# A fused attention and gated-MLP kernel: new instruction orders, and a first x load cut into single blocks on one queue

## The chip, the cores and the metric

One core of a Trainium2 chip runs the whole kernel in one launch. The metric is device time in microseconds (us), the median of several runs; a profile of one more execution goes with it. TensorE multiplies matrices, VectorE and ScalarE move results out of PSUM and do the elementwise work, GpSimd builds masks and copies some weights, SyncE issues most DMAs. Each engine runs its own list of instructions in order; semaphores tie the lists together.

## The reference, cut to what matters

x has 2048 tokens of 448 numbers (bf16). Four layers follow each other: attention (layer 0), gated MLP (1), attention (2), gated MLP (3), with the same weights for the two of a kind.

```
x = x + A(layernorm(x))     # q, k, v = x @ wqkv, 16 heads of 28;
                            # each token sees 8 keys: itself and those 2, 4, ... 14 tokens before
                            # softmax over the 8, times v, then @ wo
x = x + B(layernorm(x))     # ((x @ w_gate) * (x @ w_up)) @ w_down, 1792 wide, no activation
x = x + A(layernorm(x))
x = x + B(layernorm(x))
```

## The kernel before, in words

**Tiling.** Tokens stand in 16 blocks of 128; x stays in SBUF in x_sb, even tokens in blocks 0 to 7, odd tokens in 8 to 15, so that a dilation of 2 becomes a plain window of 8. A layer is cut into chunks of 256 or 512 tokens. SEQ interleaves the chunks of the four layers, since a chunk of the next layer can start as soon as its blocks of x are done.

**LayerNorm** (`ln_chunk`): for each block, statistics on VectorE (L580, L582), Ln and Exp on ScalarE for rstd (L583, L585), scaling on VectorE into xn_sb (L601), then a transpose. For layer 0 the transpose is done by TensorE (L611 for the first two blocks, L615) and copied out of PSUM by ScalarE or VectorE (L622, L625). For layers 1 to 3 it is a DMA transpose issued from the sync queue (L604), into xnTa for attention and xnTb for the MLP.

**Attention.** `qk_chunk`: Q and K for a chunk in four units, copied to qk (L710). `v_group`: V for pairs of query blocks of 120 tokens (L775 to L802); the last four heads of V go by DRAM (vt) and come back by a DMA transpose (L730). `attn_front`, for a group of two query blocks: masked Q (L821), an S burst of 64 small matmuls (L833), two exps on ScalarE (L842), two minima with the mask on VectorE (L849). `attn_back`: an AV burst of 64 small matmuls (L867), copies, a shuffle of the sums (L892), Ln and Exp for their reciprocal (L893, L894) and the product into oT (L905). `y_blocks`: the output projection of two blocks (Y), added to x by L922.

**MLP** (`b_chunk`): 14 gate/up units of a chunk. Each is seven steps of two matmuls on xnTb and WGU; ScalarE copies gate to g_sb (L958), VectorE multiplies with up into hT (L961). Then w_down for two blocks (on WD and hT), added to x by L922. The last two blocks of the last layer have matmuls of the full height (L973), block 14 whole, block 15 in two halves of 224 columns, added by L977 and stored.

**Steps and bursts.** Most matmuls use 64 rows, so two run at once: a step. A product of this kind has a first and a second half, in which the two row halves of the array change roles. Line L348 issues such a step. While a burst runs, steps of one other product can be issued in strips of 32 columns (L351) between its small matmuls.

**What sets the order.** The functions only declare operations, numbered as declared. ORDER (L101) gives for each engine the numbers in the order in which they are issued; `46` is one operation, `a+b/h` or `a*3/h` are strips of a set between the matmuls of burst h. BANKS gives the PSUM banks of each product. Both were written by a planner outside of the kernel, with an assumed duration for each operation. `schedule` lays the operations out by these lists, `emit` puts in a wait wherever an operation needs another engine's result or a bank that is still in use. The sync queue's DMAs stand in such a list too, so a DMA that waits holds those behind it.

**The first loads** (`load_x` and `plain_dma`, L440 to L467): x blocks 0 and 1 in one load, 2 and 3 in one, then 4 to 7, 8 to 11, 12 to 15; the Q and K columns of wqkv in four loads to a staging area (stg 0 to 3), the V columns in two (wv), the last V heads in two small ones (stv). Eight copies (L519) bring the staged weights into WQK, spaced by 32. Loads stg 0 and stg 2 are issued by ScalarE, all others by SyncE in the order x 0-1, x 2-3, x 4-7, wv, wv, stg 3, stg 1, x 8-11, x 12-15. Warm-up matmuls (L511) on zeros keep TensorE busy until the first transposes.

```
def load_x(q, lo=0, hi=4):
    two, b0 = q // 2, 4 * (q % 2)
    plain_dma("sp", x_sb[:, 4 * q + lo:4 * q + hi, :], x_par[two][:, b0 + lo:b0 + hi, :], ...)
```

Of the kernel before, what the change touches and what calls it, by code (L numbers as in the profile page):

```python
# [8 lines left out]
D = 448  # L9
# [84 lines left out]
def grp_nc(g):  # L94
# [21 lines left out]
    ),  # L116
    "act": (
# [12 lines left out]
    ),  # L130
    "dve": (
# [18 lines left out]
    ),  # L150
    "pool": (
        "23 27 34 38 39 20 28 17 19 18 43 22 21 67 68 63 24 64 25 35 26 36 31 29 30 71 73 77 75 74 32 33 40 41 42 37"
    ),
# [223 lines left out]
def build(nc, A_x, A_wqkv, A_wo, B_w_gate, B_w_up, B_w_down, out):  # L377
# [68 lines left out]
    def load_x(q, lo=0, hi=4):  # L446
        two, b0 = q // 2, 4 * (q % 2)
        plain_dma("sp", x_sb[:, 4 * q + lo:4 * q + hi, :], x_par[two][:, b0 + lo:b0 + hi, :], [("x", -1, B) for B in range(4 * q + lo, 4 * q + hi)],
                  f"d_x{q}" + "h" * (lo > 0), prio=XP_[q + (q > 0 or lo > 0)])

# [653 lines left out]
```

## Time and profile before

| | us |
|---|---|
| median of 3 runs | 390.66 (390.62 to 390.84) |
| profiled execution | 391.03 |
| its span, first to last instruction | 389.3 |
| TensorE busy in it | 379.0 |
| VectorE busy | 290.3 |
| ScalarE busy | 203.2 |
| GpSimd busy | 9.7 |

The profiled execution has 1.7 us around its span. PE is TensorE, PEld its weight loads, DVE VectorE, ACT ScalarE, POOL GpSimd, SPq the sync queue. A line of a timeline has the start, the length (of several merged instructions where a count stands behind it), engine, line, operation, what it writes and reads, and in square brackets how long the engine had stood idle before and what ended that. A matmul's busy time holds the way through the array, so two rows' lengths overlap; where a step's cost is wanted, starts are compared with starts. A wait for several things is put down to the one that came last by the profile.

### The profile page before, as it was taken

The page shows a single profiled execution, that of the slowest core. Times are in us where ns is not written, and L with a number is a line of the kernel's source. Part 1 is how long each engine was busy: PE and PEld are TensorE (multiplying, and loading weights), DVE is VectorE, ACT ScalarE, POOL GpSimd, SP SyncE. Part 2 cuts the span into 40 slices and gives each one's busy share as a digit, 9 for nine tenths or more (in the row PEclk, how much of TensorE's full clock was granted, in tenths as well). Part 3 has the DMA queues.
Part 4 walks back from the last instruction along what each step waited for, and adds up shares of the span by engine and source line. Part 5 has one row for each costly group of instructions (what it writes and reads, how often), then busy time and mean ns, then how long its engine had stood idle before and what let it go on. Part 6 is the DMA issues. An engine that isn't in the chain of part 4 may idle for free.

```text
span 389.3 us, 14648 instructions
## 1 busy us (share of the span) xinstructions
PE 379.0 (97%) x6508; PEld 212.8 (55%) x6508; DVE 290.3 (75%) x640; ACT 203.2 (52%) x388; POOL 9.7 (2%) x40
## 2 busy tenths in 40 slices
PE   7999989989999999999999999999999999999997
PEld 2644567534555554545666577645555445544774
DVE  6988879978988897677766798466997777457333
ACT  4978875574655643445344555437764723243320
POOL 4220000000000000000000000000000000000000
DMA  8756151500632113042012303430116003203012
GB/s 274 170 146 179 28 150 49 101 12 2 96 30 44 27 25 60 16 57 49 2 22 42 67 2 62 70 52 14 24 29 88 17 2 49 50 2 96 3 37 71
DMA packets 54866, 22.52 MB, mean 58 GB/s; under 512 B 44996, under 2 KB 54804, under 8 KB 54804
## 3 DMA queue, kind: packets, MB, share of 16 engines
q1 hardware_dynamic: 54372, 21.08, 26.6%
q8 instruction: 51, 0.84, 0.9%
q10 hardware_dynamic: 432, 0.52, 0.4%
q14 instruction: 11, 0.09, 0.1%
HBM read 8.54 MB, written 2.71 MB: 29 GB/s over the span
## 4 chain that ended last, share of the span: by engine, by line
PE 90%; DMA 3%; DVE 3%; ACT 2%; issue 1%; SPq 0%
PE ps L348 82%; PE ps L351 3%; PE ps L833 2%; PE ps L867 2%; ACT E_sb L842 2%; PE ps L973 1%; DMA x_sb<-in_A_x_dram 1%; DMA xnTb<-xn_sb 1%; DMA xnTa<-xn_sb 1%; DVE xn_sb L601 1%; DVE st L580 1%; DVE E_sb L849 0%; PE ps L615 0%; ACT g_sb L958 0%; ACT v_sb L802 0%
## 5 line engine op out<-in xcount | busy, mean ns | idle before, releaser
L348 PE MATMUL ps<-xnTb,WGU 64*128 64x512 bf16 (+1 forms) x1944 | 177.7, 333 | 2.6 <-DMA xnTb<-xn_sb 1.3
L348 PEld LDWEIGHTS ps<-xnTb,WGU 64*128 64x128 bf16 x1944 | 94.9, 94 | 76.0 <-DMA xnTb<-xn_sb 1.6
L958 ACT ACTIVATE g_sb<-ps 128x512 bf16<-128x512 f32 (+1 forms) x140 | 69.6, 509 | 102.4 <-PE ps L348 87.7
L961 DVE TENSOR_TENSOR hT<-g_sb,ps 128x512 bf16<-128x512 bf16 (+1 forms) x140 | 77.9, 574 | 48.0 <-ACT g_sb L958 44.2
L348 PE MATMUL ps<-WD,hT 64*128 64x448 bf16 x766 | 79.0, 350 | 0.5 <-issue 0.3
L348 PEld LDWEIGHTS ps<-WD,hT 64*128 64x128 bf16 x766 | 36.1, 94 | 32.8 <-issue 1.3
L348 PE MATMUL ps<-xnTa,WQK 64*128 64x512 bf16 (+1 forms) x488 | 52.5, 352 | 0.5 <-ACT E_sb L842 0.2
L842 ACT ACTIVATE E_sb<-ps,shift_sb 128x1024 bf16<-128x1024 f32 (+1 forms) x36 | 37.2, 1068 | 19.7 <-PE ps L833 19.4
L922 DVE TENSOR_TENSOR x_sb<-x_sb,ps 128x448 bf16<-128x448 bf16 x62 | 36.8, 614 | 11.8 <-PE ps L348 11.7
L580 DVE BATCH_NORM_STATS2 st<-x_sb 128x6 f32<-128x448 bf16 x64 | 38.4, 615 | 2.9 <-DMA x_sb<-in_A_x_dram 2.5
L601 DVE TENSOR_SCALAR xn_sb<-x_sb,mv,rstd 128x512 bf16<-128x512 bf16 (+1 forms) x64 | 35.4, 571 | 4.4 <-ACT rstd L585 4.0
L348 PEld LDWEIGHTS ps<-xnTa,WQK 64*128 64x128 bf16 x488 | 22.8, 94 | 20.5 <-PE ps L348 1.8
L348 PE MATMUL ps<-wo_g,oT 64*128 64x448 bf16 x256 | 29.2, 349 | 0.1
L849 DVE TENSOR_TENSOR E_sb<-E_sb,MK 128x1024 bf16<-128x1024 bf16 (+1 forms) x36 | 23.3, 659 | 5.4 <-ACT E_sb L842 5.2
L710 ACT ACTIVATE qk<-ps 128x1024 bf16<-128x1024 f32 (+1 forms) x25 | 22.4, 920 | 8.6 <-PE ps L348 8.3
L905 DVE TENSOR_TENSOR oT<-O_sb,R_sb 128x480 bf16<-128x480 f32 (+3 forms) x36 | 21.8, 623 | 4.0 <-ACT R_sb L894 3.8
L893 ACT ACTIVATE R_sb<-R_sb 128x480 f32<-128x480 f32 (+1 forms) x34 | 20.1, 600 | 8.5 <-DVE R_sb L892 8.5
L892 DVE STREAM_SHUFFLE R_sb<-O_sb 128x480 f32<-128x480 f32 (+1 forms) x34 | 23.3, 694 | 0.1
L348 PE MATMUL ps<-WV,xnTa 64*128 64x336 bf16 (+3 forms) x244 | 22.5, 304 | 0.1
L878 ACT ACTIVATE O_sb<-ps 128x512 f32<-128x512 f32 (+2 forms) x22 | 11.9, 562 | 17.3 <-PE ps L867 17.2
L894 ACT ACTIVATE R_sb<-R_sb 128x480 f32<-128x480 f32 (+1 forms) x34 | 20.2, 602 | 0.6
L348 PEld LDWEIGHTS ps<-wo_g,oT 64*128 64x128 bf16 x256 | 12.4, 94 | 11.8 <-PE ps L348 0.5
(64 smaller groups left out, 228.2 us busy)
## 6 DMA issues: line engine op xcount, KB each, us to landing
out_dram<-x_sb SPq DMA_DIRECT2D x15, 112.0 KB, 1.8
x_sb<-in_A_x_dram SPq DMA_DIRECT2D x3, 448.0 KB, 6.3
WGU<-in_B_w_gate_dram SPq DMA_DIRECT2D x4, 224.0 KB, 3.6
WGU<-in_B_w_up_dram SPq DMA_DIRECT2D x4, 224.0 KB, 3.7
WD<-in_B_w_down_dram SPq DMA_DIRECT2D x2, 448.0 KB, 4.1
WGU<-in_B_w_gate_dram SPq DMA_DIRECT2D x2, 336.0 KB, 5.1
WGU<-in_B_w_up_dram SPq DMA_DIRECT2D x2, 336.0 KB, 5.1
WD<-in_B_w_down_dram SPq DMA_DIRECT2D x2, 336.0 KB, 3.8
```

The costliest lines, as they stand in the source:

```text
L348: return lambda E: E.matmul(out(), lhs(), rhs(), start=start, stop=stop)
L580: sc.add("dve", one(lambda E, B=B: E.bn_stats(st6[:, B, :], x_sb[:, B, :]), ("bn", li, B)), 525.0, deps=[("x", li - 1, B)] + ([("xn", li - ...
L601: sc.add("dve", one(lambda E, B=B, dst=dst, src=src: E.tensor_scalar(dst, src, mv[:, B, 0:1], rstd[:, B:B + 1], ALU.subtract, ALU.mult), ( ...
L710: return E.activation(dst, src, ACT.Copy) if hasattr(E, "activation") else E.tensor_copy(dst, src)
L842: return E.activation(E_sb[:, slot, 2 * hp:2 * hp + 2, 0:w], ps[:, b0:b0 + 2, 0:w], ACT.Exp, bias=shift_sb[:, 0:1], scale=SCALE)
L849: return E.tensor_tensor(e, e, MK[:, kind, 0:nc].unsqueeze(1).unsqueeze(1).to_broadcast([128, 2, w // nc, nc]), ALU.min)
L892: sc.add("dve", one(lambda E: E.stream_shuffle(R_sb[:, rs, 0:w], O_sb[:, os_, 0:w], [DH] * 32), ("Rs", li, qb)), dve_est(w) + 20.0, deps=[ ...
L894: sc.add("act", one(lambda E: E.activation(R_sb[:, rs, 0:w], R_sb[:, rs, 0:w], ACT.Exp, scale=-1.0), ("R", li, qb)), act_est(w, False), de ...
L905: return E.tensor_tensor(oT[:, :, a % HALF:a % HALF + z - a], O[:, :, a - tok:z - tok], R_sb[:, rs, 0:w].rearrange("p (h n) -> p h n", h=4 ...
L922: sc.add("dve", one(lambda E: E.tensor_tensor(x_sb[:, B, :], x_sb[:, B, :], ps[:, bk[w], 0:D], ALU.add), ("x", li, B)), dve_est(D), deps=[ ...
L958: sc.add("act", one(lambda E, gs=gs, bk=bk: E.activation(g_sb[:, gs, 0:nt], ps[:, bk[0], 0:nt], ACT.Copy), ("G", li, j, fc)), act_est(nt), ...
L961: sc.add("dve", one(lambda E, gs=gs, bk=bk, fc=fc: E.tensor_tensor(hT[:, fc, hs, 0:nt], g_sb[:, gs, 0:nt], ps[:, bk[1], 0:nt], ALU.mult), ...
```

## The change

Three things change; the operations and their sizes are otherwise the same.

First, x block 0 and x block 1 are loaded by a DMA each, blocks 2 and 3 together as before. Second, stg 0 and stg 2 are issued by SyncE as well. Third, ORDER and BANKS are replaced for all engines.

```diff
-    def load_x(q, lo=0, hi=4):
+    def load_x(q, lo=0, hi=4, tag="", prio=0.0):
...
-    load_x(0, 0, 2)
-    load_x(0, 2, 4)
+    load_x(0, 0, 1, prio=-51.0)
+    load_x(0, 1, 2, "g", -49.6)
+    load_x(0, 2, 4, "h", -49.5)
...
     for c in (1, 3, 0, 2):
-        plain_dma("act" if c % 2 == 0 else "sp", stage[...], A_wqkv[...], ("stg", c), f"d_stg{c}", prio=-60 if c % 2 == 0 else -49.9)
+        plain_dma("sp", stage[...], A_wqkv[...], ("stg", c), f"d_stg{c}", prio=-49.9)
```

Since one load is new, each operation's number is one higher than before. What the new lists do, in names (from the two lists):

- SyncE's first loads: x 0, x 1, x 2-3, x 4-7, wv, stg 0, wv, stg 2, stg 1, stg 3, x 8-11, x 12-15, then the gate/up weights.
- VectorE begins with the mask memsets (L506, L507) and takes blocks 0, 1, 3, 2, 5 for its first statistics (1, 0, 3, 2, 4 before). It makes two of the eight weight copies (one before; ScalarE two, three before; GpSimd four), and a copy of V's last columns that ScalarE made.
- Layer 0, between Y of blocks 0, 1 and the first gate/up unit of layer 1: before, units of Q/K and V, the S burst of group 3 and AV of group 2. After, the same, the S burst of group 2 (before, ahead of Y) and the S burst of group 4 (before, among the gate/up units).
- Between Y of blocks 4, 5 and the second chunk's first gate/up unit: before, the S bursts of groups 4 and 5, AV of 5 and 4, w_down of blocks 0, 1, V and gate/up units. After, no S burst of 4 and 5, but that of 6, and Y of blocks 6, 7.
- Of the bursts, 19 have strips of other products inside, 46 steps in all (24 and 57 before).
- TensorE's last products: before, w_down of blocks 10 and 11, block 14, block 15 in halves. After, the two halves of block 15, block 14, then the second half of blocks 10 and 11, both of which are complete with the last step.

More of the change, by code (lines that the diff above doesn't have):

```diff
@@ L102 @@
     "pe": (
[13 rows of a table removed]
[13 rows of a table added]
     ),
     "act": (
[12 rows of a table removed]
[12 rows of a table added]
     ),
     "dve": (
[18 rows of a table removed]
[18 rows of a table added]
     ),
     "pool": (
-        "23 27 34 38 39 20 28 17 19 18 43 22 21 67 68 63 24 64 25 35 26 36 31 29 30 71 73 77 75 74 32 33 40 41 42 37"
+        "22 23 24 39 40 18 32 33 25 19 20 28 21 41 42 44 29 26 27 34 35 64 67 68 65 71 73 74 76 36 37 30 43 31 38"
     ),
     "sp": (
[5 rows of a table removed]
[5 rows of a table added]
     ),
@@ L426, in build @@
     sem_names += [f"d_x{i}" for i in range(NCH)] + ["d_stg0", "d_stg1", "d_stg2", "d_stg3", "d_wv", "d_wo", "d_wg0", "d_wg1", "d_wu0", "d_wu1", "d_wd0", "d_wd1", "d_wd2", "d_wd3", "d_out", "d_out2"]
-    sem_names += ["d_x0h"]
+    sem_names += ["d_x0g", "d_x0h"]
     sem_names += [f"d_t{li}_{j}" for li in range(4) for j in range(len(CH[li]))]
@@ L444, in build @@
     stage = hT[:].rearrange("p f s n -> p (f s n)")
-    def load_x(q, lo=0, hi=4):
+    def load_x(q, lo=0, hi=4, tag="", prio=0.0):
         two, b0 = q // 2, 4 * (q % 2)
-        plain_dma("sp", x_sb[:, 4 * q + lo:4 * q + hi, :], x_par[two][:, b0 + lo:b0 + hi, :], [("x", -1, B) for B in range(4 * q + lo, 4 * q + hi)],
-                  f"d_x{q}" + "h" * (lo > 0), prio=XP_[q + (q > 0 or lo > 0)])
-    XP_ = (-51.0, -49.5, -49.3, -48.5, -48.0)
-    load_x(0, 0, 2)
-    load_x(0, 2, 4)
+        plain_dma("sp", x_sb[:, 4 * q + lo:4 * q + hi, :], x_par[two][:, b0 + lo:b0 + hi, :], [("x", -1, B) for B in range(4 * q + lo, 4 * q + hi)], f"d_x{q}" + tag, prio=prio)
+    load_x(0, 0, 1, prio=-51.0)
+    load_x(0, 1, 2, "g", -49.6)
+    load_x(0, 2, 4, "h", -49.5)
     def wv_rows(a, lo, hi):
@@ L459, in build @@
     for c in (1, 3, 0, 2):
-        plain_dma("act" if c % 2 == 0 else "sp", stage[:, 2 * D * c:2 * D * (c + 1)], A_wqkv[CH_ROWS[c]:CH_ROWS[c] + 128, 0:2 * D], ("stg", c), f"d_stg{c}", prio=-60 if c % 2 == 0 else -49.9)
-    load_x(1)
+        plain_dma("sp", stage[:, 2 * D * c:2 * D * (c + 1)], A_wqkv[CH_ROWS[c]:CH_ROWS[c] + 128, 0:2 * D], ("stg", c), f"d_stg{c}", prio=-49.9)
+    load_x(1, prio=-49.3)
     for a in range(2):
@@ L466, in build @@
     for q in range(2, NCH):
-        load_x(q)
+        load_x(q, prio=-48.5 + 0.5 * (q - 2))
     last_x = sc.ops[-1]
```

126 rows, old and new, of tables (BANKS, ORDER) are left out of this document.

## The prediction

> **What bounds the kernel now.** I read the page first, then busy time in stretches of 10 us, then TensorE's own waits, and only then the order of time around each place where TensorE stands.
>
> ```profile
> span 389.3 us, 14648 instructions
> ...
> PE 379.0 (97%) x6508; PEld 212.8 (55%) x6508; DVE 290.3 (75%) x640; ACT 203.2 (52%) x388; POOL 9.7 (2%) x40
> ...
> PE   7999989989999999999999999999999999999997
> ```
>
> ```profile
> 0.00:10.00 10.00, 6.95 (x38) 2.67 (x38) 6.40 (x19) 4.56 (x12) 4.62 (x21) 1.00 0.83 277
> 10.00:20.00 10.00, 9.75 (x158) 6.13 (x158) 9.46 (x37) 9.22 (x24) 2.65 (x10) 1.00 0.75 175
> 20.00:30.00 10.00, 9.13 (x240) 4.80 (x236) 8.17 (x23) 7.79 (x14) 2.39 (x11) 1.00 0.57 140
> 50.00:60.00 10.00, 8.68 (x194) 6.89 (x194) 8.16 (x20) 7.37 (x16) 0.00 (x0) 1.00 0.57 159
> 70.00:80.00 10.00, 8.64 (x298) 5.13 (x270) 9.73 (x21) 5.80 (x11) 0.00 (x0) 1.00 0.41 78
> 80.00:90.00 10.00, 10.00 (x98) 4.64 (x96) 6.83 (x17) 6.70 (x12) 0.00 (x0) 1.00 0.05 9
> ```
>
> ```profile
> PE ps L348 <- DMA xnTb<-xn_sb: 1.3, 1, 1.3
> PE ps L348 <- ACT R_sb L893: 1.3, 1, 1.3
> ...
> PE ps L833 <- DVE WQK L527: 0.6, 1, 0.6
> ```
>
> The second fence gives, after the length of a stretch, the busy time of TensorE, its weight loads, VectorE, ScalarE and GpSimd, then the granted clock (1.00 throughout). TensorE is the bound from 80 us on: 10.00 of 10.00 in nearly every stretch. An order of the same matmuls can give nothing there; it can only lose. What may be won lies in three places: the first 12 us, two waits of 1.3 us before gate/up matmuls, and smaller waits between 20 and 50 us, where VectorE and ScalarE are at 8 to 9 of 10 as well. The last 2.4 us, after the last matmul, are the fourth place.
>
> **The change, part by part.**
>
> *1. The first loads.*
>
> ```profile
> 0.80 1.48 SPq L441 DMA_DIRECT2D x_sb<-in_A_x_dram  x3
> ...
> 0.85 0.95 ACTq L441 DMA_DIRECT2D hT<-in_A_wqkv_dram  x2
> ...
> 4.63 1.15 DVE L580 BATCH_NORM_STATS2 st<-x_sb 128x6 f32<-128x448 bf16 x2 [2.46 <-DMA x_sb<-in_A_x_dram]
> ...
> 8.41 0.40 DVE L601 TENSOR_SCALAR xn_sb<-x_sb,mv,rstd 128x512 bf16<-128x512 bf16 x1
> ...
> 11.58 0.27 DVE L519 COPY WQK<-hT 128x448 bf16<-128x448 bf16 x1
> ...
> 12.60 4.94 PE L348 MATMUL ps<-xnTa,WQK 64*128 64x256 bf16 x68
> ```
>
> ```profile
> GB/s 0 0 0 0 0 0 0 0 0 0 0 0 0 77 85 60 9 26 51 102 68 60 162 341 410 375 401 401 384 393 384 384 367 350 401 410 401 418 393 358
> DMA packets 681, 0.76 MB, mean 182 GB/s; under 512 B 34, under 2 KB 681, under 8 KB 681
> ```
>
> The second fence is the DMA view of 0.5 to 4.7 us, in 40 slices of 0.105 us: next to nothing until 2.8 us, then about 390 GB/s. Back from 0.76 MB at 4.7 us, some 0.06 MB had moved at 2.9 us. Now the first two x blocks (0.23 MB) share that with two weight loads from ScalarE's queue (0.46 MB), and VectorE starts at 4.63. After the change block 0 (0.115 MB) goes alone and first: its bytes are through at about 3.1 us. The old pair of first loads had its 0.46 MB through at about 3.95 and VectorE started 0.7 later; with half of that lag or all of it, block 0 is ready at 3.4 to 3.8, about 1.0 us earlier. The following blocks lie behind it at 0.3 us each, less than one statistics step (1.15/2 = 0.58), so VectorE does not wait again. Up to the third normalised block (8.41) it does the same five statistics and three scalings; the lead of 1.0 us holds there.
>
> What it then meets: all eight weight copies stand before the first Q/K matmul. Their loads go last now. But the bytes of the ten loads are the same and the DMA engines are full, so the last of them lands when it does now; two of the copies go to VectorE (one now, 0.27), behind the scaling of block 4 and ahead of block 5, and the copy of V's last columns (0.25) moves to it from ScalarE. Against this the mask memsets (0.4) move from 19 us to before the load. VectorE is the fuller engine (9.46 of 10), so I take 1.0 of lead less about 0.1: **-0.9**. Bounds: the whole earlier start and ScalarE's relief, -1.5; a last weight load that lands later because twelve issues (1.48/3 = 0.49 each) stand on one queue, +0.3. Behind them on that queue wait the gate/up weights, issued 1.5 later for three more issues; they are first read at 52.11, so that costs nothing here.
>
> [...]
>
> *2. The two waits on transposes.* The gate/up matmuls of a chunk need xnTb, which DMA transposes write.
>
> ```profile
> 45.97 2.66 SPq L604 DMA_TRANSPOSE xnTb<-xn_sb  x2
> ```
>
> ```profile
> 48.69 2.17 PE L348 MATMUL ps<-WV,xnTa 64*128 64x448 bf16 x22
> 52.11 2.47 PE L348 MATMUL ps<-xnTb,WGU 64*128 64x256 bf16 x42 [1.26 <-ACT R_sb L893]
> ```
>
> ```profile
> 72.92 3.16 SPq L604 DMA_TRANSPOSE xnTb<-xn_sb  x2
> ```
>
> ```profile
> 79.33 1.04 PE L348 MATMUL ps<-xnTb,WGU 64*128 64x512 bf16 x8 [1.30 <-DMA xnTb<-xn_sb]
> ```
>
> ```profile
> DMA to landing us min/median/max: 2.9/3.0/4.6
> ```
>
> The first wait is put down to ScalarE, but a gate/up matmul reads nothing of R_sb. The second of its two transposes was issued half way through 2.66, at about 47.3; 52.11 is 4.8 later, near the longest landing (4.6). So this is the transpose too. The second pair ends its issues at 76.1 and TensorE goes on at 79.33.
>
> After the change, between the output projection that releases the LayerNorm (Y of blocks 0, 1) and the first gate/up unit, TensorE has the same work plus two S bursts: that of group 2, which stood ahead of Y, and that of group 4, from inside the chunk. A burst is 0.62 (below, 66.98 to 67.60): 1.24 more against a wait of 1.26. VectorE puts two E minima among the scalings where it waited for rstd, which leaves the transposes where they are. **-1.25**, bounds -1.3 and 0.
>
> For the second, after Y of blocks 4, 5 the S bursts of groups 4 and 5 leave and that of group 6 and Y of blocks 6, 7 come, 8 steps of 0.19 (below): 1.5 less 0.62, so 0.9 against 1.30. The rest hangs on the issues: the last two took 3.16 here and 2.66 at the first place, 0.5 less. VectorE's list up to the last scaling holds as much as before (two additions, some four products, two statistics, four scalings, and a shuffle for a Qz). I take **-1.25**, bounds -1.3 and 0; with the slow issues again it would be -0.9.
>
> *3. Fewer bursts with other matmuls inside.* Of the S and AV bursts 24 carry strips of another product now, 57 steps; after, 19 with 46 steps (counted in the two orders).
>
> ```profile
> 66.98 0.68 PE L833 MATMUL ps<-Qz,qk 64*32 64x64 bf16 x64
> 67.60 0.94 PE L348 MATMUL ps<-xnTb,WGU 64*128 64x256 bf16 x14
> ```
>
> ```profile
> 111.42 0.26 PE L833 MATMUL ps<-Qz,qk 64*32 64x64 bf16 x16
> ...
> 112.46 0.74 PE L348 MATMUL ps<-WD,hT 64*128 64x448 bf16 x6
> ```
>
> ```profile
> 378.66 2.81 PE L348 MATMUL ps<-WD,hT 64*128 64x448 bf16 x28
> ...
> 381.41 5.51 PE L973 MATMUL ps<-WD,hT 128*128 128x448 bf16 x42
> 381.54 1.15 DVE L922 TENSOR_TENSOR x_sb<-x_sb,ps 128x448 bf16<-128x448 bf16 x2 [0.63 <-PE ps L348]
> ...
> 386.95 0.39 DVE L977 TENSOR_TENSOR x_sb<-x_sb,ps 128x224 bf16<-128x224 bf16 x1 [0.96 <-PE ps L973]
> ```
>
> Alone a burst takes 0.62. With three steps of 448 inside it takes 1.04, and these are 3 x 0.19 by themselves ((381.41-378.66)/14): 0.47 for the burst, 0.15 saved, 0.05 a step. 11 steps fewer: **+0.55**, bounds 0.3 and 0.8.
>
> *4. The end.* Now the last matmuls make half a block of 224 columns; after the change they make blocks 10 and 11, both complete at the last step, with the half blocks ahead of them.
>
> ```profile
> out_dram<-x_sb SPq DMA_DIRECT2D x3, 112.0 KB, 1.8
> ...
> out_dram<-x_sb SPq DMA_DIRECT2D x1, 56.0 KB, 1.5
> ```
>
> So 1.15 for two additions instead of 0.39, and a store of 112 KB (1.8) instead of 56 (1.5): **+0.9** (0.76 + 0.3, less 0.15 since the store row's median holds stores that queue). Bounds 0.7 and 1.1. Nothing covers it: it lies behind the last matmul.
>
> *5. New waits of the new order.* The burst of group 4, moved up to stand one V unit behind that of group 3, puts two more exps ahead of ScalarE's first evictions of gate.
>
> ```profile
> L842 ACT ACTIVATE E_sb<-ps,shift_sb 128x1024 bf16<-128x1024 f32 (+1 forms) x36 | 37.2, 1068 | 19.7 <-PE ps L833 19.4
> ```
>
> Four exps of 1.07 and one Ln (0.6) are 4.9 us from the end of group 3's burst; TensorE has behind it V (14 steps, 1.0 with its turn of halves), a burst (0.62) and three gate/up units of 7 x 0.11 = 0.77, in all 3.9, before it needs a bank that an exp or a gate eviction frees. That is a wait of up to 1.0, half of which the transposes' landing would have cost anyway: **+0.5**. Elsewhere new small waits and old ones that go (0.6 at the first S burst) are unknown, between -1.0 and +2.0; I take 0, since about as many bursts stand in as tight places in both orders.
>
> **Sum:** -0.9 - 1.25 - 1.25 + 0.55 + 0.9 + 0.5 = **-1.45** of span. The profiled execution took 391.03 with 389.3 of span; the median is 390.66, 0.37 below it. So 390.66 - 1.45 = **389.2**.
>
> **Rivals.**
> *The front gives all of it* and no new bank wait comes: -0.6 and -0.5 more, 388.1. For it: the front's 2.46 of waiting on a load. Against: VectorE at 9.46 behind it.
> *The front gives nothing*: the Q/K matmuls start at 12.6 again, since the last weight copies and x3 set it. +0.9: 390.1. For it: the copy at 11.58 stands one us ahead of 12.60 and its load is now the tenth on one queue.
> *The change doesn't do what it says*: the transposes land late again, as they do where the sync queue has other work behind them. Both waits stay, +2.5: 391.7. The point: a landing over 4.6 after issue, or VectorE's scalings 1.2 later.
> *Slower:* exps ahead of evictions. Where a burst stands two or three gate/up units before the next one, its two exps (2.1) delay the gate evictions, and TensorE, with eight banks, waits. Price up to 1.0 a place; with four such places between 50 and 130 us, +4 on -1.45: about 393. It decides from 1.45 + 0.8 = 2.25 us on, that is from three places. Against it: the old order has such bursts too and is at 10.00 from 80 us.
>
> **How the numbers follow.** Forecast 0.45; all of the front 0.20; nothing of the front 0.14; late transposes 0.06; exps 0.15. A measurement of this kernel tells about 0.2% (0.8 us) from no change. The first two are faster, 0.65; the third and half of the fourth are within it, 0.17; the rest slower, 0.18. The range reaches from 387.5, which leaves some of the second case out, to 391.7, which leaves out the exps: the unknown bounds of part 5 make it that wide.
>
> **What would show it.** First statistics on VectorE at 3.4 to 3.8 (right) or after 4.2 (wrong); the first Q/K matmul at 11.5 to 11.9; no wait over 0.5 on xnTb before 80 us; single bursts of 0.62; the span's end 3.2 us behind the last matmul instead of 2.4; a wait of about 0.5 at the first gate/up units, put down to ScalarE. A TensorE row with several 8s between 80 and 380 us would make the prediction wrong.

## The result and the profile after

The changed kernel takes 389.25 us (median of 14 runs, 388.60 to 390.24) against 390.62 for the kernel before (14 runs beside it): ratio 0.9966, 95% interval 0.9953 to 0.9978. The profiled span went from 389.3 to 387.4. The forecast was 389.2. The sum was right, in part by luck. Of its terms, the end was right in place and size, and the price of strips held but was met by an effect that I did not know. The transposes and the exps had nearly the right size, with one step each that the traces contradict, and the term of the front was right for the wrong reason. In one experiment (e8) the executions lie 2% apart together with the clock granted to TensorE (390.77 us at 1.000, 398.97 at 0.991), and its ratio rests on the shorter ones alone (3.3 us over the kernel before, against 5.0 by the median), so its median is given beside it.

From the profile page of the changed kernel: span, busy times, TensorE's 40 slices, and the DMA queue that brings in instructions (packets, MB, share).

```profile
span 387.4 us, 14498 instructions
...
PE 378.5 (98%) x6442; PEld 213.2 (55%) x6442; DVE 290.9 (75%) x643; ACT 203.1 (52%) x386; POOL 9.2 (2%) x39
...
PE   7999899999999999999999999999999999999996
...
q8 instruction: 51, 0.84, 0.9%
```

Busy time by stretch, as before (after the length: TensorE, weight loads, VectorE, ScalarE, GpSimd, granted clock):

```profile
0.00:10.00 10.00, 7.49 (x62) 3.46 (x64) 7.63 (x26) 5.09 (x13) 6.41 (x29) 1.00 0.81 267
10.00:20.00 10.00, 9.80 (x153) 5.90 (x153) 9.41 (x32) 9.42 (x23) 0.41 (x1) 1.00 0.70 169
...
50.00:60.00 10.00, 9.37 (x234) 7.54 (x228) 9.55 (x22) 9.02 (x19) 0.00 (x0) 1.00 0.51 142
70.00:80.00 10.00, 9.93 (x262) 5.68 (x260) 9.13 (x23) 6.63 (x12) 0.00 (x0) 1.00 0.57 93
```

TensorE's row of slices has one 8 behind the first slice where there were two, and the stretches from 50 to 60 (8.68 before) and 70 to 80 (8.64) are fuller. TensorE's own waits (total, times, longest) show what is left:

```profile
PE ps L832 <- issue: 0.9, 1, 0.9
PE ps L348 <- DMA WV<-in_A_wqkv_dram: 0.7, 1, 0.7
PE ps L348 <- ACT E_sb L841: 0.4, 1, 0.4
...
PE ps L348 <- issue: 0.2, 1, 0.2
```

Some line numbers of the changed kernel are one lower (L832 stands for L833). Both waits of 1.3 ahead of gate/up matmuls are gone. New are a wait on a V weight load, one on an exp, and one put down to nothing ("issue"). The order of time shows where. First the front:

```profile
2.83 1.18 DVE L579 BATCH_NORM_STATS2 st<-x_sb 128x6 f32<-128x448 bf16 x2 [0.16 <-DMA x_sb<-in_A_x_dram]
...
8.24 1.65 PE L348 MATMUL ps<-WV,xnTa 64*128 64x224 bf16 x20 [0.66 <-DMA WV<-in_A_wqkv_dram]
...
10.08 0.58 ACT L518 ACTIVATE WQK<-hT 128x448 bf16<-128x448 bf16 x1 [0.86 <-DMA hT<-in_A_wqkv_dram]
...
11.37 0.51 PE L348 MATMUL ps<-xnTa,WQK 64*128 64x256 bf16 x6
```

VectorE starts 1.80 earlier than before, more than the 1.0 forecast; but V's first matmul and the weight copies now wait for their loads, and of 1.80 a lead of 1.23 arrives at the first Q/K matmul. Then the place of the first gate/up units:

```profile
42.92 2.82 SPq L603 DMA_TRANSPOSE xnTb<-xn_sb  x2
...
46.65 0.54 PE L832 MATMUL ps<-Qz,qk 64*32 64x64 bf16 x47
...
48.09 0.26 PE L832 MATMUL ps<-Qz,qk 64*32 64x64 bf16 x17 [0.90 <-issue]
...
48.46 2.12 ACT L841 ACTIVATE E_sb<-ps,shift_sb 128x1024 bf16<-128x1024 f32 x2 [0.76 <-PE ps L832]
...
50.72 1.90 PE L348 MATMUL ps<-xnTb,WGU 64*128 64x256 bf16 x31 [0.41 <-ACT E_sb L841]
...
52.84 0.81 PE L348 MATMUL ps<-xnTb,WGU 64*128 64x256 bf16 x11 [0.22 <-issue]
```

The S burst of group 3 stops after 47 of its 64 matmuls, 1.1 us from one start to the next, and nothing in its list waits for a semaphore there. The gate/up unit no longer waits for its transposes, but for an exp. The second pair of transposes is issued until 75.35 and covered: its gate/up unit starts at 78.74 without a wait. At the end the last product and the additions of its two blocks:

```profile
72.18 3.17 SPq L603 DMA_TRANSPOSE xnTb<-xn_sb  x2
...
78.74 1.46 PE L348 MATMUL ps<-xnTb,WGU 64*128 64x512 bf16 x12
...
381.29 2.82 PE L348 MATMUL ps<-WD,hT 64*128 64x448 bf16 x28
...
384.14 1.15 DVE L921 TENSOR_TENSOR x_sb<-x_sb,ps 128x448 bf16<-128x448 bf16 x2 [1.83 <-PE ps L348]
```

The last matmul ends near 384.1, 3.3 before the end of the span; before it was 2.4.

**Where the 1.9 us of span came from.** Counted as the end of each product in the trace less the work issued ahead of it (a step at its lone price, a burst at 0.62), after less before: to the first S burst -1.5; from there to 47 us -0.7; 47 to 66 us +1.1 (transposes -1.4, the exp +0.55, pauses without a semaphore and what follows them +1.9); 66 to 81 us -1.65 (transposes -1.5); 81 us to the last matmul -0.15; behind it +0.9. Together -2.0, which leaves 0.1 open. The medians differ by less, 1.4: the profiled execution of before lies 0.4 above its median, that of after (389.22) on it.

### The profile page after: what moved, and what is told of

The parts are those of the page before. It is cut to its first block, busy times and chain, and to the rows that moved or that the text cites. A ratio compares the mean times of both kernels' runs of the same rounds, so it can differ in the third digit from the quotient of the medians.

```text
span 387.4 us, 14498 instructions
## 1 busy us (share of the span) xinstructions
PE 378.5 (98%) x6442; PEld 213.2 (55%) x6442; DVE 290.9 (75%) x643; ACT 203.1 (52%) x386; POOL 9.2 (2%) x39
## 4 chain that ended last, share of the span: by engine, by line
PE 93%; DVE 2%; ACT 1%; DMA 1%; SPq 1%; issue 1%; DVEq 0%
PE ps L348 84%; PE ps L351 2%; PE ps L866 2%; PE ps L832 2%; PE ps L972 1%; DMA hT<-in_A_wqkv_dram 1%; ACT E_sb L841 1%; SPq L441 1%; PE ps L614 0%; DVE x_sb L921 0%; DVE hT L960 0%; DVE E_sb L848 0%; ACT g_sb L957 0%; DVE qk L709 0%; DVEq L1052 0%
## 5 line engine op out<-in xcount | busy, mean ns | idle before, releaser
L348 PE MATMUL ps<-xnTb,WGU 64*128 64x512 bf16 (+1 forms) x1926 | 175.5, 333 | 1.0 <-ACT E_sb L841 0.4
L348 PE MATMUL ps<-WD,hT 64*128 64x448 bf16 x800 | 81.7, 350 | 0.2 <-DVE x_sb L921 0.2
L348 PEld LDWEIGHTS ps<-WD,hT 64*128 64x128 bf16 x800 | 38.4, 94 | 34.5 <-DVE x_sb L921 0.5
L348 PE MATMUL ps<-xnTa,WQK 64*128 64x512 bf16 (+1 forms) x498 | 54.4, 353 | 0.1
L709 ACT ACTIVATE qk<-ps 128x1024 bf16<-128x1024 f32 (+1 forms) x27 | 24.8, 927 | 13.1 <-PE ps L348 12.8
L348 PE MATMUL ps<-WV,xnTa 64*128 64x336 bf16 (+3 forms) x246 | 23.4, 305 | 0.8 <-DMA WV<-in_A_wqkv_dram 0.7
L820 DVE TENSOR_SCALAR Qz<-qk,qmask 128x960 bf16<-128x960 bf16 (+1 forms) x36 | 14.8, 452 | 7.8 <-PE ps L832 4.4
L348 PEld LDWEIGHTS ps<-wo_g,oT 64*128 64x128 bf16 x250 | 12.1, 94 | 10.9 <-PE ps L348 0.8
```

The lines of the kernel that those rows point to most:

```text
L348: return lambda E: E.matmul(out(), lhs(), rhs(), start=start, stop=stop)
L709: return E.activation(dst, src, ACT.Copy) if hasattr(E, "activation") else E.tensor_copy(dst, src)
```

## The experiments

Twelve kernels, each timed in five rounds. "Ratio" is to the kernel before, run beside it. That kernel's median lay between 390.45 and 390.93 in these groups of runs, so rows compare better by ratio than by median.

| | median us | ratio (95% interval) | span |
|---|---|---|---|
| kernel after | 389.25 | 0.9966 (0.9953 to 0.9978) | 387.4 |
| e1 loads alone | 391.34 | 1.0020 (1.0009 to 1.0031) | 391.0 |
| e2 orders alone | 389.77 | 0.9979 (0.9968 to 0.9990) | 387.4 |
| e3 old tail | 388.56 | 0.9951 (0.9938 to 0.9964) | 386.5 |
| e4 warm-ups in four | 391.33 | 1.0018 (1.0009 to 1.0026) | 389.9 |
| e5 warm-ups in two | 388.21 | 0.9925 (0.9907 to 0.9942) | 386.5 |
| e6 weights on ScalarE's queue | 390.38 | 0.9983 (0.9972 to 0.9995) | 388.3 |
| e7 no strips | 392.61 | 1.0041 (1.0026 to 1.0055) | 390.8 |
| e8 before, warm-ups in four | 395.88 | 1.0084 (1.0050 to 1.0118) | 396.3 |
| e9 e5 and e3 together | 387.39 | 0.9923 (0.9907 to 0.9938) | 386.4 |
| e10 e9, Ln behind exps | 388.39 | 0.9941 (0.9926 to 0.9956) | 387.1 |
| e11 pair in one load | 390.05 | 0.9987 (0.9978 to 0.9997) | 389.1 |
| e12 before, warm-ups in eight | 390.80 | 1.0002 (0.9989 to 1.0015) | 389.6 |

### The front: loads or orders (e1, e2, e6, e11)

e1 has the new loads and the old ORDER and BANKS (renumbered); e2 the reverse.

```diff
 e1: ORDER, BANKS of before, sync queue:
-    0-1 2-3 4-7 wv wv stg3 stg1 8-11 12-15
+    1 0 2-3 4-7 wv stg0 wv stg2 stg1 stg3 8-11 12-15
 e2: ORDER, BANKS of after, loads of before
```

> The new first loads (single blocks, block 1 ahead of block 0 because these lists take block 1 first, all on the sync queue) with the old orders and banks. Theory A, the front is worth what the trace of the changed kernel shows there (first Q/K matmul 1.2 us earlier) and nothing later takes it back: 1.0 to 1.2 us under the kernel before, ratio 0.997, first statistics near 2.9 us. Rival B, VectorE and ScalarE at 9 of 10 between 10 and 30 us take most of it back: 0 to 0.4 us under it, ratio 0.999 to 1.000, although the first statistics start as early. Rival C, the old order reads the staged weights in an order that the one queue doesn't fit: a wait on a weight load and a time over that of the kernel before.

> The new orders and banks with the old first loads (blocks 0 and 1 in one load, two of the weight loads on ScalarE's queue). Theory A, loads and orders add up: the profiled spans differ by 1.9 us, 1.1 to 1.2 of it stand in the front, so this kernel is 0.7 to 0.8 us under the kernel before, ratio 0.998. Rival B, the new orders need the early start, since they were laid out for it: 0 to 1 us over the kernel before. Rival C, the orders themselves bring the lead in the front and the loads nothing: 1.5 to 1.9 us under it, ratio 0.996.

e1 is 0.9 slower than the kernel before by the medians. Its timeline (VectorE's start, ScalarE's first weight copy, V's first matmul):

```profile
2.88 1.22 DVE L579 BATCH_NORM_STATS2 st<-x_sb 128x6 f32<-128x448 bf16 x2 [0.70 <-DMA x_sb<-in_A_x_dram]
...
9.61 0.58 ACT L518 ACTIVATE WQK<-hT 128x448 bf16<-128x448 bf16 x1 [2.66 <-DMA hT<-in_A_wqkv_dram]
...
10.81 0.46 PE L348 MATMUL ps<-WV,xnTa 64*128 64x224 bf16 x6 [1.47 <-ACT xnTa L621]
```

VectorE starts as early as planned and it helps nothing: the old order lets ScalarE copy a staged weight first (at 8.13 in the kernel before), this weight now comes late on the one queue, and the copies of the transposes stand behind it. Rival C of e1 holds. In e2 the start is late again, but the first Q/K matmul is at 11.72:

```profile
4.55 1.15 DVE L580 BATCH_NORM_STATS2 st<-x_sb 128x6 f32<-128x448 bf16 x2 [1.88 <-DMA x_sb<-in_A_x_dram]
...
11.72 0.50 PE L348 MATMUL ps<-xnTa,WQK 64*128 64x256 bf16 x6
```

From 12.60 to 11.37, 0.88 is the order's and 0.35 the loads'. In time, orders alone -0.8 (medians against those beside them: 390.45 to 389.77 is -0.7, the ratio gives -0.8), loads alone +0.8 to +0.9, both -1.3 to -1.4. They don't add up: by these rows the loads suit an order in which the V products and the first transposes come ahead of the weight copies. So e2's Theory A has the time (0.998), but not the reason. What the loads add to the new orders is read from the traces; in time the intervals of e2 and the changed kernel overlap.

e6 and e11 undo one half each of the change to the loads, under the new orders.

```diff
 e6: -        plain_dma("sp", stage[...], ...)
     +        plain_dma("act" if c % 2 == 0 else "sp", stage[...], ...)
 e11: -    load_x(0, 0, 1, prio=-51.0)
      -    load_x(0, 1, 2, "g", -49.6)
      +    load_x(0, 0, 2)
```

> The changed kernel with two of the four loads of the Q and K weights on ScalarE's queue again, the x blocks still in single loads on the sync queue. Theory A, twelve issues on one queue at 0.5 us each, the first of them of 112 KB, leave the DMA engines short and the last weight load lands 0.55 later than before (10.06 against 9.51), on which the copies at 10.08 wait: with two queues the last lands near 9.5, the first Q/K matmul comes near 11.0 instead of 11.37, and the time is 0.3 us under that of the changed kernel; first statistics near 3.3 instead of 2.83. Rival B, block 0 then shares the engines with 0.46 MB of weights, lands after 4 and the start on VectorE falls back to 4.2 or later: 0.4 us over the changed kernel. Rival C, the copies are not on the path: no change.

> The changed kernel with x blocks 0 and 1 in one load again, the weight loads still all on the sync queue, so only the split is undone. Theory A, it is the weight loads' place behind the x blocks that brings the early start (3.7 instead of 2.8 for the first statistics with them on ScalarE's queue), and the split costs: both blocks land near 3.3, everything behind them 0.5 earlier, the last weight near 9.5, the first Q/K matmul near 11.0; 0.3 us under the changed kernel, ratio 0.996 or less. Rival B, each block's early landing counts: first statistics 0.5 later, the chain of VectorE with it, 0.4 us over the changed kernel. Rival C, both cancel: no difference.

Both lose against the changed kernel, 0.7 to 1.1 us (e6) and 0.8 (e11), in the direction of Rival B and by about twice its size. VectorE starts earlier in e6 (3.74) than Rival B had it (4.2). Of e6 and of e11, VectorE's start and the first Q/K matmul:

```profile
3.74 1.27 DVE L579 BATCH_NORM_STATS2 st<-x_sb 128x6 f32<-128x448 bf16 x2 [1.07 <-DMA x_sb<-in_A_x_dram]
...
12.43 0.50 PE L348 MATMUL ps<-xnTa,WQK 64*128 64x256 bf16 x6
```

```profile
3.60 1.15 DVE L580 BATCH_NORM_STATS2 st<-x_sb 128x6 f32<-128x448 bf16 x2 [0.93 <-DMA x_sb<-in_A_x_dram]
...
7.20 0.63 DVE L580 BATCH_NORM_STATS2 st<-x_sb 128x6 f32<-128x448 bf16 x1 [0.72 <-DMA x_sb<-in_A_x_dram]
...
12.32 0.50 PE L348 MATMUL ps<-xnTa,WQK 64*128 64x256 bf16 x6
```

My theory that two queues or one load for the pair would bring the weights earlier fell with them: by the DMA records the last weight load lands at 10.2 in e6 and 10.9 in e11 (9.5 before and in e2, 10.06 after). In e11 blocks 4 to 7 land at 7.18 and VectorE waits for them; in e6 they land at 7.68. In the changed kernel and the six runs with its front they land between 5.9 and 6.6. Why these 448 KB are so much later in e6 and e11 (and at 7.04 in e1) stays open. Some 0.5 of e11's loss is not the front's: in its trace two of the pauses of the next section are longer (1.38 and 0.67 us for 1.10 and 0.40).

### The pauses without a semaphore (e4, e5, e8, e12)

The instructions of TensorE come in 51 packets of 16 KB (the q8 line above) for 13,026 entries of TensorE in the trace (matmuls, weight loads, semaphores): 255 each. I call the arrival of such a packet a refill, and I counted the entries up to each pause. The pauses at 48.09, 52.84 and one at 62.17 (there put down to a product on VectorE that ended last) are at entries 1729, 1985 and 2497 of the list: all 193 + 256 k. Between the first two the windows view counts 126 matmuls and 127 weight loads, between the second and third twice as many (a semaphore entry or two beside them):

```profile
48.08:52.75 4.67, 4.06 (x126) 2.91 (x127) 4.29 (x10) 4.29 (x5) 0.00 (x0) 1.00 0.36 83
52.83:62.16 9.33, 9.01 (x253) 7.20 (x253) 8.88 (x23) 7.69 (x20) 0.00 (x0) 1.00 0.43 122
```

e4, e5, e8 and e12 move these points without touching anything else: the warm-up matmuls are cut into narrower ones of the same columns in all.

```diff
-        one(lambda E, n=n: E.matmul(ps[:, ..., :], warm[:, 0:128], warm, ...), ("warm", n))
+        [(lambda E, n=n, i=i: E.matmul(ps[:, ..., 128*i:128*(i+1)], warm[:, 0:128], warm[:, 128*i:128*(i+1)], ...),
+          ("warm", n) if i == 3 else None) for i in range(4)]
```

> The changed kernel with each of the 16 warm-up matmuls cut into four of a quarter of the width: the same columns, 48 more matmuls with as many weight loads ahead of everything else on TensorE. It moves the points at which TensorE's instructions are refilled (every 256 or so of them) by about 96. Theory A, the pause of 1.1 us within the S burst of group 3 (46.99 to 48.09, no semaphore waited for) is a refill that is late because the DMA engines are full with transposes: the refill at 45.84 moves to about 44, ahead of the transposes, and the pause goes; 0.7 to 1.0 us under the changed kernel, or the pause stands at another matmul. Rival B, the pause belongs to that burst (what it reads is being written or moved): it stays at the same matmul, and the time is that of the changed kernel.

e4 was 2.1 slower than the changed kernel. Theory A was right that the pauses are refills and wrong on the sign: they moved, to 1985, 2241 and 9665.

```profile
49.05 0.55 PE L832 MATMUL ps<-Qz,qk 64*32 64x64 bf16 x48
50.25 0.26 PE L832 MATMUL ps<-Qz,qk 64*32 64x64 bf16 x16 [0.65 <-issue]
...
54.94 1.26 PE L348 MATMUL ps<-xnTb,WGU 64*128 64x256 bf16 x20 [0.89 <-issue]
```

```profile
264.43 0.23 PE L866 MATMUL ps<-E_sb,v_sb 64*32 64x64 bf16 x9 [1.53 <-issue]
```

The S burst of group 3 runs through, that of group 4 stops, and an AV burst at 264 us, where the transposes of LayerNorm are far off (DMA share 0.02 from 260 to 265 us). So those transposes are not needed for a pause. The DMA view of the changed kernel from 45.8 to 46.9 us has one packet of instructions:

```profile
q8 instruction: 1, 0.02, 5.4%
```

By its record it starts at 45.84, and TensorE goes on at 48.09. In all the traces a refill's packet starts about 0.8 us (median; 0.7 in the traces of the two kernels) after TensorE has passed the point 256 entries ahead of the one that it serves, with packets and points paired in order, and where TensorE paused it went on 2.2 to 3.0 us after that start (once 3.7). In three pauses the stretch and the pause together came to 3.2 to 3.6 us: 2.49 us in the changed kernel gave 1.10, 2.66 in e4 gave 0.84, 1.46 there gave 1.72. So 256 entries in less than that tended to end in a pause of the rest. The start of the packet counts as well, and it varies, from 2.0 us ahead of TensorE's passing to 3.6 behind it. In the changed kernel 256 entries of 2.42 us at 292 us end in no pause, since their packet started 1.2 ahead of TensorE's passing. The pauses at 52.84 and 62.17 stand behind stretches of 4.3 and 4.5 us, since their packets started 2.3 and 2.6 after the point. e2, e3 and e6 have the same points, and the one at 62.17 is missing there. A lone burst is 128 entries in 0.62 us, and the stretch of 2.49 holds one and most of a second (from 44.49 and from 46.65). From the trace of the changed kernel I worked out the sum of these rests for each shift; 32 entries was the best.

> The changed kernel with each of the 16 warm-up matmuls cut into two of half the width: 16 more matmuls with their weight loads, 32 instructions. Theory A, TensorE's instructions come in refills of 256; in all the traces so far the pauses without a semaphore stand at instruction 193 + 256 k, and only where TensorE ran the 256 before it in less than about 3.45 us. Moving the points by 32 leaves one stretch of 256 under 3.45 (3.36) instead of three places that cost 1.10, 0.49 and 0.40: 1.9 us less, some 387.4 (ratio 0.992), and up to 0.5 more where the wait of 0.41 on the exps of group 3 ahead of the first gate/up unit was a sequel of the pause. Rival B, the pauses belong to the bursts and the transposes: no change, 389.2, or they move as irregularly as with the cut in four: over 390.

```profile
46.98 0.68 PE L832 MATMUL ps<-Qz,qk 64*32 64x64 bf16 x64
...
50.18 0.50 PE L348 MATMUL ps<-xnTb,WGU 64*128 64x256 bf16 x6 [0.41 <-ACT E_sb L841]
```

e5: 388.21, ratio 0.9925, so 1.0 (medians) to 1.6 (ratios) less, of 1.9 forecast. All three pauses are gone; a new one of 0.44 stands near 30 us, where the stretch takes 4.0 us and the refill started 1.6 after the point, while gate/up weights were being loaded. Since the third pause also comes and goes at unmoved points, e5 shows the move best for the first. The stretch of 3.36 us that was left passed without a pause. The wait on the exp did not go with the pause, so that half of the expectation fell.

> The kernel before with its warm-up matmuls cut in four, 96 instructions more, as in the run of the changed kernel that was 2.1 us slower. Theory A (a stretch of 256 instructions under 3.45 us ends in a pause of the rest): the stretches of the trace of before, moved by 96, sum to 5.7 us of pauses instead of 0.5, so about 5 us slower, 395.7, ratio 1.013. Rival B, the pauses hang on what the bursts and the transposes of the new order do: no change against the kernel before, since its own list has only 0.9 us of them.

e8: median 395.88 (12 executions from 390.77 to 398.97), near the 395.7 that was expected, though with such a spread the match is partly luck; its profiled execution (398.1) has pauses of 0.7 to 2.2 us at five points, 7.4 in all, more than the 5.7 worked out, and something else behind the longest ones (the granted clock is the third figure from the end):

```profile
216.00:221.00 5.00, 3.20 (x168) 2.15 (x166) 3.87 (x13) 1.15 (x4) 0.00 (x0) 0.97 0.43 79
221.00:226.00 5.00, 5.00 (x38) 2.19 (x36) 0.66 (x2) 3.02 (x6) 0.00 (x0) 0.68 0.38 52
226.00:231.00 5.00, 5.00 (x74) 3.36 (x72) 4.72 (x11) 0.70 (x3) 0.00 (x0) 1.00 0.00 0
...
295.00:300.00 5.00, 4.06 (x50) 1.89 (x52) 4.69 (x12) 2.42 (x5) 0.00 (x0) 0.66 0.68 121
```

After a pause of 1.80 in a burst at 219 us the granted clock is 0.68 over five us, which costs up to 1.6 more by my estimate (five us less 0.68 of them), and a clock of 0.66 follows the pause of 1.89 that ends at 295.94. The cut in four adds 2.1 us to the new order (e4) and 3.3 to 5 to the old one (e8), and the cut in two takes 1.0 to 1.6 from the new one (e5). Rival B of e8 fell. What speaks most for refills as the cause is the place: all the pauses of TensorE that the fourteen traces put down to "issue" stand at 193 + 256 k, to within two entries, wherever the cuts have moved that point. How long a pause becomes, the length of the stretch alone does not tell.

> The kernel before with its warm-up matmuls cut in eight, 224 instructions more: by the stretches of its trace this leaves one under 3.45 us (3.20 at 67 us), so its own pauses at the refills (0.48 and 0.62 near 295 us, 0.2 elsewhere) go. It asks how much of the difference between the two kernels is luck with the refill points. Theory A, the pauses cost what they show: 0.8 to 1.1 us under the kernel before, ratio 0.9975, and the two orders, each at points that suit it, differ by 1.7 us. Rival B, near 295 us TensorE would have waited anyway: within 0.3 us of the kernel before. Rival C, the refills come closer to the front's full DMA engines, and a pause like the 1.72 and 0.67 with the cut in four shows up near 25 us: 1 us or more over it.

e12: 390.80, no difference. Its pauses near 295 us are gone: from the second gate/up wait to the last w_down step of 64 rows it takes 298.43 us (378.92 less 80.49) against 299.33 in the kernel before.

```profile
52.50 0.72 PE L348 MATMUL ps<-xnTb,WGU 64*128 64x256 bf16 x10 [1.47 <-DMA xnTb<-xn_sb]
...
80.49 1.69 PE L348 MATMUL ps<-xnTb,WGU 64*128 64x512 bf16 x14 [1.75 <-DMA xnTb<-xn_sb]
...
378.92 2.81 PE L348 MATMUL ps<-WD,hT 64*128 64x448 bf16 x28
```

But the two waits on xnTb are 1.47 and 1.75 (1.26 and 1.30 before), and 0.2 is lost near 30 us: the 0.9 was given back there. The time is what Rival B had, for another reason; Theory A's price of the pauses is seen in the trace and not in the time. What made those transposes later was not tried.

### The price of strips (e7)

```diff
-531*3/521 ... 1360*2/1399      (19 bursts with strips inside)
+531 521 ... 1360 1399          (the burst, then the other product)
```

> The changed kernel with all 19 interleaved bursts undone: each burst alone, the product whose strips it carried behind it in full height steps, 46 steps in all. The prediction's price, 0.05 us a step, makes it 2.3 us slower than the changed kernel, about 391.5. Theory A, from the positions of the products in the traces of before and after: interleaving gains next to nothing (between 0.1 lost and 0.05 won for each burst), so within 0.9 us of the changed kernel once the pauses at the refills, which move since 46 steps have 12 instructions fewer each, are taken out by the trace.

392.61, 3.36 over the changed kernel (2.9 by the ratios). The waits of TensorE show more pauses than the 0.9 and 0.2 of the changed kernel:

```profile
PE ps L831 <- issue: 0.9, 1, 0.9
PE ps L347 <- issue: 0.5, 1, 0.5
PE ps L865 <- issue: 0.5, 2, 0.3
```

Summed at the refill points from start to start these are 3.1 against 2.0, so 1.1 of 3.36 is theirs, and 2.3 over 46 steps is 0.05 a step (0.04 by the ratios). That is the prediction's price; Theory A, read from positions of products in two traces with different pauses, fell.

### The end (e3, e9) and the exp (e10)

```diff
 e3, TensorE: -1516 1517 1587 1590 1584 1518 1519     (additions and stores likewise)
              +1516 1517 1518 1519 1584 1587 1590
 e10, ScalarE: -577 281 380 381
               +577 380 381 281                        (281: the Ln of group 3; 380, 381: its exps)
```

> The changed kernel with the old order at the end: the second half of w_down of blocks 10 and 11 ahead of block 14 and the two halves of block 15, additions and stores likewise. Theory A, the end costs what stands behind the last matmul, 3.24 us of span after it instead of 2.37: this kernel is 0.85 us under the changed one, or 0.99 with one turn of matmul shape fewer; ratio to the kernel before 0.994. Rival B, the additions of blocks 10 and 11 then hold back those of block 15 on VectorE, or the last stores queue: 0.3 us or less under the changed kernel, ratio 0.996.

> The changed kernel with the warm-up matmuls in two halves and the old order at the end together. Theory A, the two add up, since one acts before 65 us and the other behind the last matmul: ratio 0.990 (0.9925 of the halves alone less 0.0022), 387 us. Rival B, one of the two was a matter of the chip or the round: 0.9925 or more.

> As the run before, and on ScalarE the Ln of group 3's sums (0.60) moved from ahead of the two exps of group 3's S burst to behind them. Theory A, the wait of 0.41 ahead of the first gate/up unit is for a bank that the second of these exps frees, and the Ln holds it back by 0.4 after the burst's end: the wait goes, 0.35 to 0.5 us under the run before. Rival B, the gate evictions behind group 4's exps are next in line and TensorE waits there instead: no difference.

In e3 the last addition is over at 384.5, the span at 386.5, 0.9 less than after; the medians differ by 0.7. Behind the last matmul it has 2.4 us instead of 3.3, as Theory A had it; in time the intervals of the two kernels overlap.

```profile
384.11 0.39 DVE L976 TENSOR_TENSOR x_sb<-x_sb,ps 128x224 bf16<-128x224 bf16 x1 [0.95 <-PE ps L972]
```

e9 puts both repairs together: 387.39, the lowest median of all, below both kernels. Its ratio (0.9923) does not tell it from e5 (0.9925), so that the two add up is likely from the traces (2.4 us behind the last matmul, no pause in the S burst of group 3), not shown by the times.

In e10 the wait on the exp stays as it was:

```profile
46.55 0.33 PE L832 MATMUL ps<-Qz,qk 64*32 64x64 bf16 x31
...
48.19 0.41 PE L832 MATMUL ps<-Qz,qk 64*32 64x64 bf16 x33 [1.31 <-issue]
...
48.70 2.12 ACT L841 ACTIVATE E_sb<-ps,shift_sb 128x1024 bf16<-128x1024 f32 x2 [1.85 <-PE ps L832]
...
50.96 2.84 PE L348 MATMUL ps<-xnTb,WGU 64*128 64x256 bf16 x42 [0.40 <-ACT E_sb L841]
```

The exps now start as soon as the burst ends, and still end 0.1 ahead of the gate/up matmul: two exps of 1.06 are longer than the V unit and the burst that TensorE has in between. Both theories fell; the Ln was not the main cause (in e5, with the Ln ahead, the exps started 0.3 after the burst's end instead of 0.1). The pause in the S burst came back, 1.3 us at a stretch of 3.36 us that had just passed in e5: its refill started 2.4 us after TensorE had passed the point, that of e5 1.3 ahead of it. That makes e10 the slower one, and its time says nothing on the Ln.

## Why the prediction was right, and where it was not

| step | forecast | measured |
|---|---|---|
| 1 front | -0.9 by the loads | -1.5 at the first S burst: orders -1.1, loads -0.4 (e2) |
| 2 first and second wait on xnTb | -1.25, -1.25 | -1.4, -1.5 |
| 3 fewer strips | +0.55 | 0.05 a step (e7); no net loss from 81 us on |
| 4 the end | +0.9 | +0.9 in the trace, 0.7 in time (e3) |
| 5 exps ahead of gate | +0.5 | +0.55 |
| small waits, 22 to 47 us | 0 | -0.7 |
| refills of instructions | not known | +1.9 |

**1. The front** failed as a working, not as a number. "The bytes of the ten loads are the same and the DMA engines are full, so the last of them lands when it does now": it lands at 10.06, not 9.51, and the copies at 10.08 wait for it. "The following blocks lie behind it at 0.3 us each": blocks 0 and 1 land at 2.81 and 3.36, 0.55 apart. The two loads were issued 0.45 apart, and in the eight traces with single blocks all on the sync queue they land 0.40 to 0.59 apart. So the pace of issues, which the prediction left out here, is enough to explain the distance; whether the rate has a part in it is not shown. VectorE started 0.6 to 1.0 earlier than forecast, lost a third of its lead to loads, and what the orders did in the front (0.88 at the first Q/K matmul, e2) I had counted as nothing but a relief of ScalarE. With the old orders the loads are a loss of 0.9 (e1): a load's gain is a property of the order that reads it.

**2. The transposes** were both covered: no wait over 0.5 on xnTb before 80 us. For the second, one step was wrong: it counted on issues 0.5 shorter, and they took 3.17 as before, with which its own sum had -0.9. The wait went because the issues ended 0.7 earlier (75.35 instead of 76.08) and TensorE came to its gate/up unit 0.7 later (78.74, against 79.33 less 1.30).

**3. The strips.** The price held. That nothing is lost from 81 us on is because the kernel before had refill pauses there, 0.48 and 0.62 near 295 us, worth 0.9 together (e12 against before), which the new list does not have. The step was right and its net was met by an effect outside the prediction. So a busy row of 10.00 was not the proof that an order can give nothing there.

**4. The end** was right in place and size.

**5. The exps** were right in size and near in place, by another wait than the one worked out: TensorE waits ahead of the first gate/up unit for the exps of group 3, whose bank that unit takes, and not after three units for those of group 4 ahead of the gate evictions (e5, e10). The match of the size is partly luck.

**The unknown.** The bounds of -1.0 to +2.0 held both what was missing: -0.7 of small waits and +1.9 of refills. The rival of exps at three or more places did not come: from 80 us on TensorE waits for VectorE once, 0.2 us, and never for ScalarE.

So 389.2 was met by luck in the sum: +1.9 that was not foreseen stood against about -0.6 more in the front, -0.4 more at the transposes, -0.7 of small waits, and 0.55 of strips that other pauses paid. Of the span the forecast was -1.45, and -1.9 was measured; of the medians -1.4. The signs named ahead came for the waits, the exps and the end; the first statistics (2.83) and the first Q/K matmul (11.37) came earlier than their ranges.

## What to carry to other kernels

Before crediting an order with half a percent, count where the engine's instruction refills fall: a few more instructions ahead of everything moved the time of these two kernels by -1.6 to +5 us. A load made earlier is worth what the order behind it can use, so change both and test each alone. Terms worked out from rows held here when the same operation stood in the trace at the same kind of place; the one for DMA engines assumed full failed: the last weight load landed at 10.06, not at 9.51.

## What the runs showed of the hardware

- TensorE's instructions arrived about 256 at a time (51 packets of 16 KB for 13,026 entries, pauses at 193 + 256 k), and the packet for the next 256 started about 0.8 us (median) after the point before had been passed, with single ones from 2.0 ahead of it to 3.6 behind it; one that came 3.4 behind stood beside DMA transposes (before, near 296 us). In nearly all pauses TensorE went on 2.2 to 3.0 us after the packet's start. 256 instructions in under 3.2 to 3.6 us often ended in a pause (2.49 in the changed kernel, 1.46 and 2.66 in e4, 3.13 in the kernel before), but 2.42 us did not where the packet was early, and 4.3 to 5.4 us did where it was late. In the stretch of 2.49 stood one lone burst of 64 small matmuls with 64 weight loads, 0.62 us, and most of a second.
- After pauses of 1.80 and 1.89 us inside bursts (e8) the granted clock stood at 0.68 and 0.66 over the next five us; after one of 1.53 (e4) it stayed at 1.00.
- Two loads of 112 KB, issued 0.45 us apart on one queue, landed 0.55 apart (2.81 and 3.36; 0.40 to 0.59 over eight traces), not much less than the last three weight loads of 224 KB (8.79, 9.38 and 10.06).
